# Subtractions that make the low halves of weights, and of sums of weights: from GpSimd to VectorE

## The chip, the cores and the metric

One NeuronCore of a Trainium2 chip runs the whole program. The time is that of one execution on the device in microseconds, and the kernel before was run three times: 880.67, 881.78 and 882.65 us, median 881.78.

## The reference

Three parts follow each other over 2304 tokens.

```python
phi = lambda x: exp(h - max(h)) / sqrt(m)        # h = x @ omega.T - |x|^2 / 2
num, den = phi(q) @ (phi(k).T @ v), phi(q) @ sum(phi(k))
x = num / (den + 1e-6)                           # attention, 4 x 8 heads, 576 x 64, 128 features
g = softplus(x @ w_in)                           # 512 -> 2048
y = g @ w_out                                    # 2048 -> 512
out = ((y @ w1) * (y @ w2)) @ w3 @ w_out2        # 512 -> 1024 -> 1024 -> 512
```

q and k are scaled by 64^(-1/4) first. All inputs and outputs are float32, and the products are wanted at that accuracy.

## The kernel before, in words

**Numbers in two halves.** Each operand of a large product is held as a high half (a cast to `float32r`) and a low half (the operand minus its high half), and a product is three matmuls: high by high, high by low, low by high (`mm3`, line 89; all matmuls carry line 87). The high half is a cast on ScalarE (`hi_` line 176, `hi_t` line 189, `dhi` line 581), the low half a subtraction: on GpSimd for the weights (`lo_` line 181), for the sums of weights (`lo_t` line 193) and for the attention's operands (`split`, line 263); on VectorE for the activations of the narrowing products (`dlo`, line 582), the activations of the widening ones (line 433) and the folded weight (line 794).

**Jobs.** A `Job` brings one block of weights in. It loads it as 64-bit words (line 120, issued from ScalarE's queue) and rebuilds the values from two 32-bit words: a `relu` on ScalarE (line 127), then four steps on VectorE (lines 130, 136, 143, 150), all in a tile `f` of the pool `T_`, which has four slots. The blocks of `w_in` (8 jobs) and of `w1` and `w2` (8 jobs, 1024 columns each) also get four sums of their quarters in a second tile `t` of that pool (lines 157, 160, 163), because the widening products go by a scheme with seven block products instead of eight. Such a job then makes `thi`, `tlo` (1024 columns), `hi`, and two pieces of `lo` (256 and 512 columns). The other jobs make `hi` and one `lo`: `w_out` (ten blocks of 768 columns and one of 512), `wo` (eight of 512, the last into the tile `spare`, line 715) and `w3` (eight of 1024). The halves lie in slots that come free when the matmuls of an earlier block are done.

**Stages.** Attention runs until about 155 us, and two jobs of `w_in` are done within it. The first widening product (`Up1`, from about 155 to 345 us) takes 24 quads, one for each block of `w_in` and third of the tokens; a quad has seven products of six matmuls, whose sums VectorE makes from PSUM (`add`, line 475: `u2`, `u3`, `c22`, `c21`, `c12`), which frees the banks, and ScalarE's softplus follows (line 507). The first narrowing product (`down`, lines 565 to 612, until about 575 us) multiplies 16 slices of `g` by `w_out` for five chunks of tokens; within it the jobs of `wo`, `w3` and six of `w1`/`w2` run (four of these only up to their values, which are spilled to memory and reloaded later), and `w3` is multiplied by `wo` (`fold`, line 719). The second widening product (`Up2`, until about 780 us) multiplies the two results by each other on VectorE (line 530: `c<-c,c` with both inputs in SBUF, `c<-ps,c` with one in PSUM), and the second narrowing product ends the kernel.

**What sets the order.** Job steps stand in a list `queue`; `step(rate)` (line 234) emits some of them after each product or slice, so that they are spread over the matmuls. A step that needs free slots waits for a count (`take`, line 105). In the list the step `lo_t` follows `hi_t`, then come `hi_` and `lo_`, and only then the next block's `relu` (lines 195 to 213). A scheduler of the framework then puts the instructions of each engine into one fixed order when the program is built, from program order and a plan of times; sums, softplus, `dhi`, `dlo` and results are marked urgent (`tc.high_priority(URGENT)`) and go ahead of what was emitted up to 300 places earlier if they are ready in that plan. On the chip every engine takes its instructions in that order, each after a wait for what it reads and for the slot that it writes.

Of the kernel before, what the change touches and what calls it, by code (L numbers as in the profile page):

```python
# [19 lines left out]
F32 = mybir.dt.float32  # L20
# [4 lines left out]
ALU = mybir.AluOpType  # L25
# [37 lines left out]
def body(ctx: ExitStack, tc: tile.TileContext, q, k, k_rest, v, v_rest, om_t, w_in, w_out, w12, w3, wo, out):  # L63
    nc = tc.nc
# [47 lines left out]
    class Job:  # L112
# [65 lines left out]
        def lo_(self):  # L178
            self.lo = self.place("lo")
            for a, b in ((0, 256), (512, 1024)) if self.sums else ((0, self.n),):  # L180
                nc.gpsimd.tensor_tensor(  # L181
                    out=self.lo[:, a:b], in0=self.f[:, a:b], in1=self.hi[:, a:b].bitcast(F32), op=ALU.subtract
                )
            self.done = True
# [5 lines left out]

        def lo_t(self):
            self.tlo = self.place("tlo")
            nc.gpsimd.tensor_tensor(out=self.tlo, in0=self.t, in1=self.thi.bitcast(F32), op=ALU.subtract)  # L193

        def splits(self):
            if self.sums:
# [686 lines left out]
```

## Time and profile before

| | us |
|---|---|
| median of three runs | 881.78 |
| lowest and highest | 880.67, 882.65 |
| the profiled execution | 882.83 |
| its span, first to last instruction | 881.0 |
| TensorE (PE) busy | 850.9 |
| VectorE (DVE) busy | 597.6 |
| ScalarE (ACT) busy | 381.8 |
| GpSimd (POOL) busy | 177.9 |

An engine's busy time is the time in which it runs instructions; those that only wait, branch or issue a DMA are not in it. A duration includes time in which a started instruction is held up. Idle time is put down to what ended it. The granted clock is a share of TensorE's full speed. Times in the views count from the start of the span.

### The profile page before, as it was taken

What the parts mean: (1) busy time and instruction counts of PE and PEld (TensorE: products, weight loads), DVE (VectorE), ACT (ScalarE), POOL (GpSimd) and SP (SyncE); (2) the same over time, 40 slices, a digit from 0 to 9 for tenths busy, and PEclk for the clock granted to TensorE, in tenths of its full rate; (3) what the DMA queues carried; (4) which work ended last, traced back from release to release, by engine and by line L of the source; (5) the groups of instructions that cost most, each with busy time, mean ns of one, the idle gap of its engine ahead of it and who ended that gap; (6) DMA issues with size and microseconds to landing.
All of it is one profiled execution on the core that took longest, in us unless ns stands there. A gap on an engine that the chain in (4) does not pass through costs nothing.

```text
span 881.0 us, 14617 instructions
## 1 busy us (share of the span) xinstructions
PE 850.9 (97%) x5496; PEld 763.9 (87%) x5496; DVE 597.6 (68%) x932; ACT 381.8 (43%) x796; POOL 177.9 (20%) x110
## 2 busy tenths in 40 slices
PE   8999989999899999999989999999999999999998
PEld 7888878989899988788768888899999999988887
DVE  5678788888775587887986686169986655563322
ACT  6678978563443455444433332164321111132221
POOL 3524420022222243222311211100042222000000
PEclk9999999999999999999989999999999999999999
DMA  8623534565443457766676664064322211364432
GB/s 298 240 84 97 156 99 133 186 215 181 156 149 133 150 195 266 239 190 237 203 275 235 238 219 161 31 204 137 126 102 78 78 54 55 128 201 144 143 120 96
DMA packets 72535, 141.68 MB, mean 161 GB/s; under 512 B 7056, under 2 KB 39952, under 8 KB 69392
## 3 DMA queue, kind: packets, MB, share of 16 engines
q1 hardware_dynamic: 65984, 102.99, 35.0%
q10 hardware_dynamic: 6480, 37.75, 12.5%
q8 instruction: 43, 0.70, 0.3%
q14 instruction: 28, 0.23, 0.1%
HBM read 94.05 MB, written 46.66 MB: 160 GB/s over the span
## 4 chain that ended last, share of the span: by engine, by line
PE 53%; DVE 4%; DMA 2%; issue 1%; ACT 1%; POOL 0%; ACTq 0%; DVEq 0%; POOLq 0%
PE ps L87 53%; DMA raw<-in_w 1%; DVE f L150 1%; DMA dn<-gd 1%; DVE f L143 1%; DVE dlo L582 0%; DVE f L130 0%; DMA raw<-in_wo 0%; DVE f L136 0%; ACT dhi L581 0%; DVE c L475 0%; DVE u L475 0%; ACT hi L176 0%; POOL tlo L193 0%; ACT f L127 0%
## 5 line engine op out<-in xcount | busy, mean ns | idle before, releaser
L181 POOL TENSOR_TENSOR lo<-f,hi 128x512 fp32r<-128x512 f32 (+3 forms) x58 | 93.2, 1621 | 195.1 <-ACT hi L176 162.5
L582 DVE TENSOR_TENSOR dlo<-dn,dhi 128x512 fp32r<-128x512 f32 (+1 forms) x120 | 89.0, 752 | 62.6 <-ACT dhi L581 44.1
L87 PE MATMUL ps<-dlo,hi 128*128 128x512 f32 (+1 forms) x320 | 120.8, 378 | 4.8 <-DVE dlo L582 4.8
L87 PE MATMUL ps<-dhi,hi 128*128 128x512 f32 (+1 forms) x320 | 119.1, 375 | 1.2 <-DVE c L475 0.7
L87 PE MATMUL ps<-dhi,lo 128*128 128x512 f32 (+1 forms) x320 | 120.2, 376 | 0.0
L193 POOL TENSOR_TENSOR tlo<-t,thi 128x1024 fp32r<-128x1024 f32 x16 | 39.7, 2478 | 301.6 <-ACT thi L189 195.5
L581 ACT CAST dhi<-dn 128x512 fp32r<-128x512 f32 (+1 forms) x120 | 67.3, 577 | 65.5 <-DVE dlo L582 30.7
L87 PEld LDWEIGHTS ps<-dlo,hi 128*128 128x128 f32 x320 | 60.8, 190 | 17.7 <-DVE dlo L582 6.2
L130 DVE SCALAR_TENSOR_TENSOR f<-raw,f 128x1024 f32<-128x1024 f32 (+2 forms) x43 | 51.0, 1188 | 33.2 <-ACT f L127 33.0
L87 PEld LDWEIGHTS ps<-dhi,hi 128*128 128x128 f32 x320 | 60.5, 189 | 14.6 <-DVE c L475 1.8
L475 DVE TENSOR_TENSOR c<-ps,u 128x384 f32<-128x384 f32 x144 | 71.6, 550 | 0.9
L87 PEld LDWEIGHTS ps<-dhi,lo 128*128 128x128 f32 x320 | 60.9, 190 | 11.7
L482 ACT COPY p<-ps 128x384 f32<-128x384 f32 x48 | 22.9, 477 | 103.8 <-PE ps L87 99.1
L475 DVE TENSOR_TENSOR u<-ps,p 128x384 f32<-128x384 f32 x48 | 26.6, 555 | 60.8 <-PE ps L87 60.8
L127 ACT ACTIVATE f<-raw 128x1024 f32<-128x1024 f32 (+2 forms) x43 | 42.5, 993 | 49.7 <-DMA raw<-in_w 25.4
L176 ACT CAST hi<-f 128x1024 fp32r<-128x1024 f32 (+2 forms) x42 | 38.5, 922 | 57.6 <-PE ps L87 30.8
L507 ACT ACTIVATE c<-c 128x384 f32<-128x384 f32 x72 | 35.2, 524 | 63.3 <-DVE c L475 59.0
L309 DVE TENSOR_REDUCE nmax<-ps 128x4 f32<-128x512 f32 x72 | 48.2, 683 | 19.4 <-PE ps L87 10.0
L87 PE MATMUL ps<-dlo,w34h 128*128 128x512 f32 (+1 forms) x160 | 59.6, 373 | 0.0
L87 PE MATMUL ps<-dhi,w34l 128*128 128x512 f32 (+1 forms) x160 | 59.6, 373 | 0.0
L87 PE MATMUL ps<-dhi,w34h 128*128 128x512 f32 (+1 forms) x160 | 59.1, 373 | 0.0
L150 DVE SCALAR_TENSOR_TENSOR f<-raw,f 128x1024 int32<-128x1024 int32 (+2 forms) x43 | 53.1, 1236 | 0.6
(147 smaller groups left out, 2163.5 us busy)
## 6 DMA issues: line engine op xcount, KB each, us to landing
gd<-c SPq DMA_DIRECT2D x96, 192.0 KB, 2.4
dn<-gd SPq DMA_DIRECT2D x64, 256.0 KB, 3.6
raw<-in_w ACTq DMA_DIRECT2D x16, 1024.0 KB, 6.0
pd<-c SPq DMA_DIRECT2D x48, 192.0 KB, 1.9
dn<-pd SPq DMA_DIRECT2D x32, 256.0 KB, 3.2
raw<-in_w_out ACTq DMA_DIRECT2D x10, 768.0 KB, 4.1
raw<-in_w_in ACTq DMA_DIRECT2D x6, 1024.0 KB, 5.0
rawq<-in_q SPq DMA_DIRECT2D x18, 256.0 KB, 3.8
```

The costliest lines, as they stand in the source:

```text
L87: nc.tensor.matmul(out=o, lhsT=a, rhs=b, start=start, stop=stop, **kw)
L127: nc.scalar.activation(out=self.f, in_=self.words(1, F32), func=AF.Relu, scale=-1.0)
L130: nc.vector.scalar_tensor_tensor(out=self.f, in0=self.words(1, F32), scalar=SMALLEST, in1=self.f, op0=ALU.max, op1=ALU.max)
L150: nc.vector.scalar_tensor_tensor(out=fi, in0=self.words(0, I32), scalar=29, in1=fi, op0=ALU.logical_shift_right, op1=ALU.bitwise_or,)
L176: nc.scalar.copy(out=self.hi, in_=self.f)
L181: nc.gpsimd.tensor_tensor(out=self.lo[:, a:b], in0=self.f[:, a:b], in1=self.hi[:, a:b].bitcast(F32), op=ALU.subtract)
L193: nc.gpsimd.tensor_tensor(out=self.tlo, in0=self.t, in1=self.thi.bitcast(F32), op=ALU.subtract)
L309: nc.vector.tensor_reduce(out=nmax, in_=pj, axis=AX.X, op=ALU.max, negate=True)
L475: nc.vector.tensor_tensor(out=z, in0=bank, in1=y, op=ALU.add)
L507: nc.scalar.activation(out=dst, in_=src, func=AF.Softplus)
L581: nc.scalar.copy(out=hi, in_=got[m])
L582: nc.vector.tensor_tensor(out=lo, in0=got.pop(m), in1=hi.bitcast(F32), op=ALU.subtract)
```

## The change

The subtractions `lo_` and `lo_t` of `Job` are issued on VectorE. Their operands, shapes, tiles and place in the list of steps are the same. The subtraction in `split`, line 263, stays on GpSimd.

```diff
--- before.py
+++ after.py
@@ -178,7 +178,7 @@
         def lo_(self):
             self.lo = self.place("lo")
             for a, b in ((0, 256), (512, 1024)) if self.sums else ((0, self.n),):
-                nc.gpsimd.tensor_tensor(
+                nc.vector.tensor_tensor(
                     out=self.lo[:, a:b], in0=self.f[:, a:b], in1=self.hi[:, a:b].bitcast(F32), op=ALU.subtract
                 )
             self.done = True
@@ -190,7 +190,7 @@
 
         def lo_t(self):
             self.tlo = self.place("tlo")
-            nc.gpsimd.tensor_tensor(out=self.tlo, in0=self.t, in1=self.thi.bitcast(F32), op=ALU.subtract)
+            nc.vector.tensor_tensor(out=self.tlo, in0=self.t, in1=self.thi.bitcast(F32), op=ALU.subtract)
 
         def splits(self):
             if self.sums:
```

## Rows read from the trace of the kernel before

**Rows 1.** The page: busy time, share and instructions of each engine over the span.

```profile
PE 850.9 (97%) x5496; PEld 763.9 (87%) x5496; DVE 597.6 (68%) x932; ACT 381.8 (43%) x796; POOL 177.9 (20%) x110
```

**Rows 2.** Busy time by stretch; then granted clock, DMA share and GB/s.

```profile
66.00:110.00 44.00, 43.32 (x586) 37.96 (x584) 35.12 (x91) 39.31 (x113) 20.48 (x15) 1.00 0.42 126
308.00:352.00 44.00, 41.19 (x219) 37.52 (x218) 36.23 (x52) 24.18 (x45) 16.30 (x8) 1.00 0.68 227
638.00:660.00 22.00, 21.22 (x122) 20.89 (x121) 19.60 (x33) 5.21 (x7) 10.18 (x6) 1.00 0.29 102
231.60:234.90 3.30, 3.30 (x12) 3.30 (x11) 2.45 (x5) 1.23 (x2) 0.00 (x0) 0.50 0.96 308
445.00:449.90 4.90, 4.90 (x12) 3.84 (x13) 3.29 (x4) 3.01 (x5) 2.37 (x1) 0.50 0.93 335
```

**Rows 3.** Timeline of TensorE: start, duration, instruction; in brackets idle time and what ended it.

```profile
230.08 0.45 PE L87 MATMUL ps<-xs1h,thi 128*128 128x384 f32 x1 [2.30 <-DVE c L475]
...
263.07 0.44 PE L87 MATMUL ps<-xs1h,thi 128*128 128x384 f32 x1 [1.55 <-DVE c L475]
...
287.13 0.44 PE L87 MATMUL ps<-xs1h,thi 128*128 128x384 f32 x1 [1.95 <-DVE c L475]
...
444.95 0.79 PE L87 MATMUL ps<-dlo,hi 128*128 128x512 f32 x1 [4.30 <-DVE dlo L582]
...
641.39 0.45 PE L87 MATMUL ps<-xs2h,tlo 128*128 128x384 f32 x1 [0.78 <-POOL tlo L193]
```

**Rows 4.** GpSimd by line and shape: count, busy us, mean ns; idle time before.

```profile
L193 POOL TENSOR_TENSOR tlo<-t,thi 128x1024 fp32r<-128x1024 f32 x16 | 39.7, 2478 | 301.6 <-ACT thi L189 195.5 <-PE ps L87 106.2
L181 POOL TENSOR_TENSOR lo<-f,hi 128x512 fp32r<-128x512 f32 x24 | 36.3, 1511 | 29.7 <-ACT hi L176 29.7
...
L181 POOL TENSOR_TENSOR lo<-f,hi 128x768 fp32r<-128x768 f32 x10 | 20.5, 2064 | 40.0 <-ACT hi L176 26.3 <-PE ps L87 13.6
L181 POOL TENSOR_TENSOR lo<-f,hi 128x1024 fp32r<-128x1024 f32 x8 | 20.4, 2553 | 90.3 <-ACT hi L176 71.3 <-PE ps L87 13.4 <-issue 5.5
L181 POOL TENSOR_TENSOR lo<-f,hi 128x256 fp32r<-128x256 f32 x16 | 16.7, 1045 | 35.1 <-ACT hi L176 35.1
```

**Rows 5.** VectorE by line and shape, forms that show an unhindered duration.

```profile
L143 DVE SCALAR_TENSOR_TENSOR f<-raw,f 128x1024 int32<-128x1024 int32 x24 | 29.4, 1225 | 0.4
...
L160 DVE TENSOR_TENSOR t<-f,t 128x256 f32<-128x256 f32 x16 | 6.7, 420 | 0.2
...
L433 DVE TENSOR_TENSOR xa22l<-xq,xa22h 128x768 fp32r<-128x768 f32 x6 | 5.7, 950 | 0.0
...
L794 DVE TENSOR_TENSOR w34l<-w,w34h 128x512 fp32r<-128x512 f32 x8 | 5.4, 687 | 5.1 <-ACT w34h L791 5.1
```

**Rows 6.** The same view of VectorE, three long forms and one to compare.

```profile
L582 DVE TENSOR_TENSOR dlo<-dn,dhi 128x512 fp32r<-128x512 f32 x96 | 79.4, 834 | 52.8 <-ACT dhi L581 39.1 <-PE ps L87 10.2 <-DMA wd<-w 3.0
...
L130 DVE SCALAR_TENSOR_TENSOR f<-raw,f 128x1024 f32<-128x1024 f32 x24 | 33.8, 1408 | 16.6 <-ACT f L127 16.5
...
L530 DVE TENSOR_TENSOR c<-c,c 128x384 f32<-128x384 f32 x24 | 21.8, 906 | 0.0
...
L530 DVE TENSOR_TENSOR c<-ps,c 128x384 f32<-128x384 f32 x24 | 13.2, 551 | 0.0
```

**Rows 7.** Timeline of VectorE and GpSimd at two places: start, duration, instruction.

```profile
224.58 3.43 POOL L193 TENSOR_TENSOR tlo<-t,thi 128x1024 fp32r<-128x1024 f32 x1 [11.62 <-ACT thi L189]
...
226.13 2.96 DVE L150 SCALAR_TENSOR_TENSOR f<-raw,f 128x1024 int32<-128x1024 int32 x1
...
438.05 2.99 DVE L130 SCALAR_TENSOR_TENSOR f<-raw,f 128x1024 f32<-128x1024 f32 x1
```

**Rows 8.** Timeline of ScalarE in the first widening product.

```profile
283.32 0.90 ACT L127 ACTIVATE f<-raw 128x768 f32<-128x768 f32 x1 [3.07 <-POOL lo L181]
```

**Rows 9.** VectorE by line and shape in the stretch 308 to 352 us.

```profile
L130 DVE SCALAR_TENSOR_TENSOR f<-raw,f 128x768 f32<-128x768 f32 x6 | 7.2, 1215 | 4.6 <-ACT f L127 4.5
L150 DVE SCALAR_TENSOR_TENSOR f<-raw,f 128x768 int32<-128x768 int32 x5 | 7.0, 1401 | 0.1
```

## The prediction

> **What bounds the kernel now.** I read the page's busy times first: TensorE is busy 850.9 of 881.0 us, VectorE 597.6, GpSimd 177.9 [rows 1]. So the time is TensorE's work plus 30.1 us in which it stands still; only that, and stretches in which its clock is low, can be won, while VectorE has 283 us to spare on the whole. Then I read stretches [rows 2] and the places where TensorE waits [rows 3]. Of the 30.1 us, 12.8 sit in the first widening product (2.30, 1.55, 1.95 us, and a second of the 1.95 kind one job, 24 us, later: four stalls, all ended by a sum on line 475 that frees a PSUM bank), at the end of the first narrowing product (4.30 us, ended by a low half on line 582) and at the start of the second widening one (0.78 us, ended by GpSimd's own `tlo`) [rows 3]. The other 17 are the two ends of the kernel, the attention stage and the first operands, and I leave them as they are. After two of them the granted clock is 0.50, the lower of its two levels (1.2 instead of 2.4 GHz), in at least 3.3 and 4.9 us of work [rows 2]; before each fall TensorE had stood still for over 2 us.
>
> **What is moved.** 16 sums of weights (1024 columns), and of line 181: 16 of 256, 24 of 512, 10 of 768 and 8 of 1024 columns [rows 4], with one more of 512 into the `spare` tile: 75 instructions. No DMA moves, no queue is changed but these two. GpSimd loses 39.7 + 36.3 + 20.5 + 20.4 + 16.7 = 133.6 us and keeps only the splits of line 263. On VectorE a subtraction of two SBUF tensors takes 0.687 us for 512 columns, 0.950 for 768 and 0.420 for 256; for 1024 there is no subtraction, and the nearest is line 143, two SBUF inputs as well, 1.225 [rows 5]. Added to VectorE: 24 x 1.225 + 25 x 0.687 + 10 x 0.950 + 16 x 0.420 = 29.4 + 17.2 + 9.5 + 6.7 = 62.8 us.
>
> **What VectorE gets back.** Some of its instructions are longer than others of their shape. `dlo` at 512 columns averages 834 ns where the same operation on line 794, in a stretch without GpSimd, takes 687: 96 x 0.147 = 14.1 us. `c<-c,c` averages 906 where `c<-ps,c`, with one input in PSUM, takes 551: 24 x 0.355 = 8.5. Line 130 at 1024 columns averages 1408 against 1225: 4.4 [rows 5, 6]. In the stretch 308 to 352 the 768-column forms of lines 130 and 150 average 1215 and 1401 against 950: 6 x 0.265 + 5 x 0.451 = 3.8 [rows 9]. The single rows say when: line 150 at 226.13 takes 2.96 us while GpSimd's `tlo`, begun at 224.58, runs to 228.01; line 130 at 438.05 takes 2.99 [rows 7]. VectorE is held while GpSimd reads SBUF. Together 30.8 us at least come back, so VectorE's busy time grows by at most 32 us, to about 629: by itself that reaches nothing on the path.
>
> **What it does to TensorE's stalls, one by one.**
> - At 227.8 to 230.1: line 150 stands directly ahead of the sums that free the bank. Alone it takes 1.22, so they come 1.74 us earlier. A stall of 0.6 should leave the clock up: half of the 3.3 us at 0.50 comes back as well, 1.65 [rows 2, 3, 7]. Gain 3.4; bounds 0 (a moved `tlo` of 1.22 takes the freed place) and 4.0 (2.30 and the clock).
> - At 261.5 and twice as at 285.2: here the chain runs over tile slots. ScalarE's `relu` for the next job waits for the slot that GpSimd's low half still reads (3.07 us at 283.32 [rows 8]), line 130 on VectorE waits for `relu`, and the sums that TensorE needs are queued behind line 130. A `tlo` is 2.48 - 1.23 = 1.25 shorter on VectorE, the two `lo` 1.05 + 1.51 - 0.42 - 0.69 = 1.45 [rows 4, 5]. I take 1.2 of the 1.55, and both 1.95 whole, as 1.25 + 1.45 is more: 5.1. Bounds 0 and 5.45.
> - At 440.7: the VectorE order is line 130 (2.99), 136, 143, 150 and then the `dlo` that TensorE waits for. The hold of 1.77 goes, a `lo` of 1.22 comes in: 0.5 gained. Bounds: -1.2 (no hold goes, the `lo` comes), and 4.30 + 4.9 x 0.5 = 6.7 if the stall and its low clock go altogether [rows 2, 3, 7].
> - At 640.6: `tlo` itself is what TensorE waits for. It is shorter, but must now find a place between VectorE's urgent sums; I take 0, bounds +0.8 (the stall goes) and -1.1 (three sums and two products of 0.55 us, overlapping to 2.4 us, go ahead of it, less the 1.25).
>
> **What it costs.** In the attention stage two jobs are split, 2 x (1.225 + 0.420 + 0.687) = 4.7 us more on VectorE, where it is 80% busy and TensorE almost full (35.1 and 43.3 of 44 us [rows 2]). Cover is thin; I take 2.0, bounds 0 and 4.7. Every moved instruction follows a cast on ScalarE, and now all of VectorE's queue stands behind it if the cast is late. GpSimd could wait there at no cost. The nearest rows for that: 0.0 behind the operand cast (line 433) and 5.1 us over 8 (0.64 each) on line 794 [rows 5]; for 59 casts that is 0 to 38 us of VectorE idling, out of 283, and I cost it at 0 where TensorE has work in hand, since the urgent sums are ordered ahead. If that cover goes, the next late thing is a sum on line 475 again.
>
> Sum: -3.4 - 5.1 - 0.5 + 0 + 2.0 = -7.0 us. The profiled execution took 882.83 (span 881.0 and 1.8 around it), 1.05 above the median 881.78. So 881.8 - 7.0 = **874.8 us**.
>
> **Rivals.** *VectorE becomes the bound in the stages where it is full* (slower). 308 to 352 holds eight 768-column halves: 36.2 + 7.6 = 43.8 of 44 us if the held time did not come back, 40.0 with the 3.8 of [rows 2, 9]; 638 to 660 two jobs: 19.6 + 4.7 = 24.3 of 22. The mechanism: in each job of the first widening product the `tlo`, behind its cast, stands ahead of the sums that free the banks, in the very place that the hold leaves. Then the four stalls stay and each of the six jobs there adds 1.22: +7.3, with the 2.0 of the attention stage +9.3, so 891; it decides from the point where the wait of the `xs1h` matmuls for line 475 is above 2.3 us per job. For it: the stalls are there now, with VectorE not full. Against it: the hold cannot be foreseen by an order fixed at build time, while a planned instruction can. The Trainium skill has a rule on this side (Perfetto Trace Analysis, Optimizing Scalar/DVE Operations): "if DVE is saturated, offloading some work to Scalar (or even GPSIMD) may make sense", though it adds that between those two it might not help because they share a read port; by the first half the time would come out as in this rival, by the second as in my sum, and the lengthened rows speak for the second.
>
> *The late stall goes too* (faster). The 1024-column jobs ahead of 438 lose holds like the 1.77 there, the `dlo` comes in time and the clock stays up: another 6.7 - 0.5 = 6.2 off, 868.6. For it: 4.30 us of stall behind one held instruction. Against it: four job instructions stay queued ahead of that `dlo`, and a fifth joins them.
>
> *Nothing to measure.* Only the hold at 226 counts (-3.4), attention and the start at 640 take 2.0 and 1.1 back: 881.5. The slot chain would then be followed by the next wait, `relu` for its load.
>
> **Chances.** My forecast 0.46, the late stall gone too 0.19, nothing 0.13, VectorE the bound 0.22. About 0.2% (1.8 us) is what a measurement of this kernel can tell from no change. So faster 0.65, same 0.13, slower 0.22. The likeliest case alone spans 871 to 879, from the bounds of attention (0 to 4.7) and of 440 and 640. The range goes down to 866, past the 868.6 by the bounds of the first two stalls, and up to 887, which takes in half of the slower rival.
>
> **What would show it.** Right: GpSimd down to about 43 us; VectorE 615 to 630; `dlo` at 512 columns near 690 ns and `c<-c,c` near 550; no stall over 1 us in 200 to 310, no 0.50 clock near 231; line 127 no longer waiting for a low half. Wrong: stalls ended by line 475 as long as before, with a moved subtraction ahead of the sum; long idling of VectorE ahead of `lo` or `tlo` for a cast; or new stalls with a low clock in 308 to 352 or 638 to 660.

## The result, and the profile after

The changed kernel took 868.15 us (median of six runs, 865.56 to 873.72), the kernel before 881.43 us in its six runs beside it: a ratio of 0.985, with an interval of [0.9829, 0.9871], so 13.2 us less. A second set of runs on another chip gave 868.18 against 883.39, 0.9817 [0.9791, 0.9843], 16.1 us less. The ratios are taken over all runs of both kernels and differ a little from those of the medians. From here on a difference in us is a ratio's distance from 1 times 882, so 0.001 is 0.9 us.

The profiled execution took 865.56 us, with a span of 863.7; it is the shortest of the six, so the two traces lie 17.3 us apart and not 13.2. Its busy times, on the page:

```profile
PE 845.2 (98%) x5496; PEld 760.6 (88%) x5496; DVE 605.7 (70%) x1007; ACT 381.8 (44%) x796; POOL 43.5 (5%) x35
```

Against [rows 1], GpSimd lost 134.4 us and VectorE gained 8.1, for 75 instructions. TensorE's idle time fell from 30.1 to 863.7 - 845.2 = 18.5 us, by 11.6 of those 17.3 us; its work at the low clock, where half the time is lost, went from 8.5 us (near 231 and after 443) to 6.8.

VectorE by line and shape (count, busy us, mean ns, idle before), to set against [rows 5, 6]:

```profile
L582 DVE TENSOR_TENSOR dlo<-dn,dhi 128x512 fp32r<-128x512 f32 x96 | 65.4, 689 | 50.3 <-ACT dhi L581 28.2 <-PE ps L87 13.9 <-issue 5.9
L130 DVE SCALAR_TENSOR_TENSOR f<-raw,f 128x1024 f32<-128x1024 f32 x24 | 30.1, 1255 | 22.6 <-ACT f L127 22.6
...
L193 DVE TENSOR_TENSOR tlo<-t,thi 128x1024 fp32r<-128x1024 f32 x16 | 19.6, 1228 | 9.4 <-ACT thi L189 9.4
L181 DVE TENSOR_TENSOR lo<-f,hi 128x512 fp32r<-128x512 f32 x24 | 16.5, 686 | 1.3 <-ACT hi L176 1.3
L136 DVE TENSOR_SCALAR f<-f 128x1024 int32<-128x1024 int32 x24 | 16.4, 686 | 0.2
...
L530 DVE TENSOR_TENSOR c<-c,c 128x384 f32<-128x384 f32 x24 | 13.2, 549 | 0.0
L181 DVE TENSOR_TENSOR lo<-f,hi 128x1024 fp32r<-128x1024 f32 x8 | 9.8, 1222 | 0.8 <-ACT hi L176 0.8
...
L181 DVE TENSOR_TENSOR lo<-f,hi 128x768 fp32r<-128x768 f32 x10 | 9.5, 950 | 2.1 <-ACT hi L176 2.1
...
L181 DVE TENSOR_TENSOR lo<-f,hi 128x256 fp32r<-128x256 f32 x16 | 7.5, 467 | 2.8 <-ACT hi L176 2.8
```

The moved work is 19.6 + 16.5 + 9.8 + 9.5 + 7.5 = 62.9 us, and 0.7 for `spare`. What pays for it stands in the other rows: `dlo` 689 ns instead of 834, `c<-c,c` 549 instead of 906, line 130 1255 instead of 1408.

TensorE by stretch (busy PE, PEld, DVE, ACT, POOL, granted clock, DMA share, GB/s). The work that the kernel before has at 440 to 462 and at 638 to 660 runs at about 432 to 448 and 623 to 645 here, so the last two stretches are set earlier than in [rows 2]:

```profile
66.00:110.00 44.00, 41.94 (x522) 36.10 (x523) 35.10 (x89) 34.23 (x96) 11.36 (x9) 0.96 0.35 107
198.00:308.00 110.00, 110.00 (x637) 110.00 (x636) 89.54 (x144) 52.38 (x99) 0.00 (x0) 1.00 0.54 183
308.00:352.00 44.00, 39.81 (x191) 34.25 (x190) 39.10 (x57) 23.54 (x40) 0.00 (x0) 0.96 0.68 232
426.00:448.00 22.00, 22.00 (x96) 17.73 (x95) 16.09 (x20) 9.05 (x14) 0.00 (x0) 1.00 0.88 290
622.70:644.70 22.00, 22.00 (x129) 22.00 (x128) 20.89 (x39) 5.44 (x7) 0.00 (x0) 1.00 0.30 102
```

Every stall of [rows 3] is gone. In 198 to 308, where the kernel before has PE busy for 104.20 of 110 us, it never stops, and there is no low clock near 231 or where the stall of 440 was. But two stretches of the first half are worse than they were, and in both the clock is now at 0.96. The timeline of TensorE shows the stalls that are new:

```profile
88.39 1.10 PE L368 MATMUL ps<-ident,qp 128*128 128x128 f32 x4 [1.26 <-ACT qp L314]
...
341.92 0.50 PE L87 MATMUL ps<-dlo,hi 128*128 128x512 f32 x1 [2.22 <-DVE dlo L582]
```

After each of them the clock was 0.50 for 3.4 us (from 90.5 and from 343.1). The second trace of this kernel (e12_after) has both stalls again, 1.26 and 2.21 us, but no low clock behind the first. The stall at 339.7 is a price of the change, as the timelines of ScalarE and VectorE ahead of it show:

```profile
337.84 1.14 ACT L581 CAST dhi<-dn 128x512 fp32r<-128x512 f32 x2
...
338.45 0.95 DVE L181 TENSOR_TENSOR lo<-f,hi 128x768 fp32r<-128x768 f32 x1
339.32 0.95 DVE L143 SCALAR_TENSOR_TENSOR f<-raw,f 128x768 int32<-128x768 int32 x1
340.30 0.96 DVE L150 SCALAR_TENSOR_TENSOR f<-raw,f 128x768 int32<-128x768 int32 x1
341.18 1.29 DVE L582 TENSOR_TENSOR dlo<-dn,dhi 128x512 fp32r<-128x512 f32 x2
```

`dhi` was ready at 338.98, but `dlo` began at 341.18. A moved `lo` and two steps of the next job stood ahead of it on VectorE, none of them lengthened.

### The profile page after: what moved, and what is told of

The parts are those of the page before. It is cut to its first block, busy times and chain, and to the rows that moved or that the text cites. A ratio compares the mean times of both kernels' runs of the same rounds, so it can differ in the third digit from the quotient of the medians.

```text
span 863.7 us, 14514 instructions
## 1 busy us (share of the span) xinstructions
PE 845.2 (98%) x5496; PEld 760.6 (88%) x5496; DVE 605.7 (70%) x1007; ACT 381.8 (44%) x796; POOL 43.5 (5%) x35
## 4 chain that ended last, share of the span: by engine, by line
PE 81%; DVE 4%; DMA 3%; issue 1%; ACT 1%; SPq 0%; DVEq 0%; ACTq 0%
PE ps L87 80%; DMA xq<-xd 2%; PE ps L368 1%; PE ps L398 1%; DMA raw<-in_w_in 1%; DVE s L423 1%; DVE c L475 0%; DMA dn<-gd 0%; DMA gd<-c 0%; DVE f L143 0%; DVE u L475 0%; DVE nmax L309 0%; DVE xt L389 0%; DVE lo L181 0%; DVE dlo L582 0%
## 5 line engine op out<-in xcount | busy, mean ns | idle before, releaser
L582 DVE TENSOR_TENSOR dlo<-dn,dhi 128x512 fp32r<-128x512 f32 (+1 forms) x120 | 74.8, 636 | 60.2 <-ACT dhi L581 33.5
L482 ACT COPY p<-ps 128x384 f32<-128x384 f32 x48 | 22.8, 475 | 99.5 <-PE ps L87 78.0
L130 DVE SCALAR_TENSOR_TENSOR f<-raw,f 128x1024 f32<-128x1024 f32 (+2 forms) x43 | 45.7, 1066 | 27.0 <-ACT f L127 26.9
L309 DVE TENSOR_REDUCE nmax<-ps 128x4 f32<-128x512 f32 x72 | 48.1, 682 | 18.5 <-PE ps L87 11.9
L181 DVE TENSOR_TENSOR lo<-f,hi 128x512 fp32r<-128x512 f32 (+3 forms) x58 | 42.0, 745 | 6.9 <-ACT hi L176 6.9
L143 DVE SCALAR_TENSOR_TENSOR f<-raw,f 128x1024 int32<-128x1024 int32 (+2 forms) x43 | 45.3, 1056 | 0.6
L150 DVE SCALAR_TENSOR_TENSOR f<-raw,f 128x1024 int32<-128x1024 int32 (+2 forms) x43 | 44.9, 1046 | 0.4
```

The costliest lines, as they stand in the source:

```text
L130: nc.vector.scalar_tensor_tensor(out=self.f, in0=self.words(1, F32), scalar=SMALLEST, in1=self.f, op0=ALU.max, op1=ALU.max)
L143: nc.vector.scalar_tensor_tensor(out=fi, in0=self.words(1, I32), scalar=-0x40000000, in1=fi, op0=ALU.bitwise_and, op1=ALU.bitwise_or,)
L150: nc.vector.scalar_tensor_tensor(out=fi, in0=self.words(0, I32), scalar=29, in1=fi, op0=ALU.logical_shift_right, op1=ALU.bitwise_or,)
L181: nc.vector.tensor_tensor(out=self.lo[:, a:b], in0=self.f[:, a:b], in1=self.hi[:, a:b].bitcast(F32), op=ALU.subtract)
L309: nc.vector.tensor_reduce(out=nmax, in_=pj, axis=AX.X, op=ALU.max, negate=True)
L582: nc.vector.tensor_tensor(out=lo, in0=got.pop(m), in1=hi.bitcast(F32), op=ALU.subtract)
```

## The experiments

All of them were run in five rounds beside the kernel before. The theory was that GpSimd holds VectorE up while it reads SBUF, and that this delay, not the duration of GpSimd's own work, is what TensorE's stalls were made of. The main rival was the chain of slots: a low half on GpSimd keeps `f` or `t` longer, so that `relu` and all that follows it start late.

### Reading or only writing: e3_again and e8_hold

Both are the changed kernel with GpSimd work put behind each moved subtraction: in the one GpSimd reads SBUF (it takes the low half from itself, which leaves zeros), in the other it only writes, and keeps the slot that much longer.

```diff
 # e3_again, behind each lo (and the same with tlo)
+nc.gpsimd.tensor_tensor(out=self.lo[:, a:b], in0=self.lo[:, a:b].bitcast(F32),
+                        in1=self.lo[:, a:b].bitcast(F32), op=ALU.subtract)
 # e8_hold, behind each lo (and the same with t)
+nc.gpsimd.memset(self.f[:, a:b], 0.0)
```

> The changed kernel, with one GpSimd subtraction of the old shape added behind each moved one: it takes the finished low half from itself in place, so the low halves of the weights are zero here and those terms are left out of the output. It reads SBUF as the old GpSimd work did, but not the tiles f and t, so ScalarE's relu does not wait for it. Theory 'hold' (VectorE is held while GpSimd reads SBUF, and that delayed the sums and dlo): dlo and the bit steps again reach 2.5 to 3.0 us, VectorE's busy time rises by 30 to 45 us, and at least 5 of the 13 us are lost: 873 to 882. Rival 'slots' (what cost time was the slow release of the four slots of f and t): relu still doesn't wait, 866 to 871 whatever VectorE's durations do.

> The changed kernel, with a GpSimd memset over f and over t behind each moved subtraction. It only writes, and keeps each slot of f and t some 1 us longer, about as long as the old GpSimd subtraction did. The output is the full one. Theory 'hold': two-input VectorE instructions keep their unhindered durations (dlo near 690 ns) and the time stays at 866 to 870. Rival 'slots': relu waits for GpSimd again, stalls of 1 to 2 us of TensorE between 200 and 310 us return, 873 to 878.

With the reads: 881.04 us, 0.9973 [0.9952, 0.9994], so nearly all that the change had won was gone. Its page, and two rows of VectorE by line and shape:

```profile
PE 849.1 (97%) x5496; PEld 761.2 (87%) x5496; DVE 654.7 (75%) x1007; ACT 381.9 (44%) x796; POOL 161.1 (18%) x110
```

```profile
L582 DVE TENSOR_TENSOR dlo<-dn,dhi 128x512 fp32r<-128x512 f32 x96 | 68.8, 726 | 40.4 <-ACT dhi L581 26.8 <-PE ps L87 8.7 <-issue 4.7
L130 DVE SCALAR_TENSOR_TENSOR f<-raw,f 128x1024 f32<-128x1024 f32 x24 | 32.9, 1370 | 17.0 <-ACT f L127 17.0
```

GpSimd was busy 117.6 us more than in the changed kernel, and VectorE, with the same 1007 instructions, 49.0 us more (30 to 45 had been expected). Timelines of GpSimd, VectorE and TensorE at the longest new stall:

```profile
348.33 2.11 POOL L183 TENSOR_TENSOR lo<-lo 128x768 fp32r<-128x768 f32 x1 [5.62 <-DVE lo L181]
...
349.15 2.10 DVE L150 SCALAR_TENSOR_TENSOR f<-raw,f 128x768 int32<-128x768 int32 x1
...
351.91 0.80 PE L87 MATMUL ps<-dlo,hi 128*128 128x512 f32 x1 [3.35 <-DVE dlo L582]
```

Line 150 took 2.10 us here, under GpSimd's read, against 0.96 at 340.30 in the changed kernel, and it stood ahead of the `dlo` that TensorE wanted. Three things have to be said against this run, though. Some 55 of VectorE's 1007 places in the order differ from the changed kernel. At 198.25 TensorE waits 0.95 us for GpSimd's second `tlo` itself. And most of the time was lost at other places than those where the change had won it (TensorE by stretch):

```profile
198.00:308.00 110.00, 108.31 (x610) 107.10 (x609) 96.47 (x140) 51.28 (x95) 27.92 (x18) 1.00 0.48 165
308.00:352.00 44.00, 35.94 (x188) 31.75 (x186) 41.72 (x55) 21.53 (x39) 13.29 (x8) 1.00 0.67 226
```

None of the four stalls near 230 to 310 came back, nor that of 440; 308 to 352, where PE is busy 39.81 us in the changed kernel and 41.19 in the kernel before, lost more than any other stretch. So the run shows that GpSimd's reads lengthen VectorE's instructions and that this can cost as much as the change had won. It does not show what the stalls of the kernel before were made of.

With the writes alone: 867.77 us, 0.9823 [0.979, 0.9857], the time of the changed kernel. VectorE was busy 606.9 us, with 16 places in its order changed. Two rows by line and shape:

```profile
L582 DVE TENSOR_TENSOR dlo<-dn,dhi 128x512 fp32r<-128x512 f32 x96 | 65.2, 688 | 46.9 <-ACT dhi L581 27.0 <-PE ps L87 11.5 <-issue 5.5
...
L193 POOL MEMSET t<- 128x1024 f32 x16 | 15.3, 956 | 325.2 <-DVE tlo L193 325.2
```

So 48.2 us of GpSimd work that only writes lengthened the instructions with two SBUF inputs by next to nothing; line 136, which has a single tensor input, gained some 1.0 us in all (703 instead of 686 ns at 1024 columns). A slot kept about 1 us longer cost nothing in the changed kernel, but from 198 to 310 us no `relu` waited for it either, so the run does not tell what the longer keeping cost in the kernel before. The Trainium skill (SBUF — State Buffer, Who interferes with whom) has the same division: a VectorE instruction with two SBUF inputs contends with a GpSimd instruction that reads SBUF, and not with one that only writes it. These two runs agree with it: `dlo` 726 and 688 ns.

### A shorter read in the same order: e4_nochain and e10_chain

Both are the kernel before, with GpSimd taking the high half twice instead of the value and the high half (so the low halves are zero). In e4_nochain `f` and `t` come free with the casts; e10_chain adds a one-column `memset` of them behind each, which ties them to GpSimd again.

```diff
-out=self.lo[:, a:b], in0=self.f[:, a:b], in1=self.hi[:, a:b].bitcast(F32), op=ALU.subtract
+out=self.lo[:, a:b], in0=self.hi[:, a:b].bitcast(F32), in1=self.hi[:, a:b].bitcast(F32), op=ALU.subtract
 # e10_chain only
+nc.gpsimd.memset(self.f[:, a:a + 1], 0.0)
```

> The kernel before, with GpSimd's subtraction reading the high half twice in place of f (or t) and the high half: same engine, shape and reads of SBUF, but f and t are free as soon as the cast on ScalarE is done. The low halves of the weights are zero and those terms are left out. Theory 'hold' alone: VectorE's long durations stay, the stall at 440 us with its low clock stays, at most 1 to 3 us are won: 878 to 881. Rival 'slots': the three stalls that my working put down to slots (5.1 us) go, 872 to 877. If both are at work, something between, 875 to 879.

> The kernel e4_nochain (GpSimd subtracts the high half from itself) with one more GpSimd instruction behind each subtraction: a memset of one column of f or t, so that the slots of f and t are again free only when GpSimd is done. VectorE's instructions stand in the very order of the kernel before. The low halves of the weights are zero here. Theory 'slots' (on GpSimd the late release of the slots is what costs, through relu and what is queued behind it on VectorE): the 13 us that e4_nochain won are lost again, 879 to 884, relu waits 2 to 3 us for GpSimd and the four stalls near 230 to 310 us are back. Rival 'lighter reads' (e4_nochain was faster because GpSimd reads one tensor and not two, 2.0 against 2.5 us, and so holds VectorE less): 867 to 872.

e4_nochain took 869.06 us, 0.9838 [0.9804, 0.9872], faster than all its forecasts. It did more than cut the chain: GpSimd is faster when both operands are the same tensor, as the row of the second run shows too, 1983 ns for `tlo` against 2478 [rows 4]:

```profile
L193 POOL TENSOR_TENSOR tlo<-thi 128x1024 fp32r<-128x1024 f32 x16 | 31.7, 1983 | 303.6 <-ACT thi L189 175.2 <-PE ps L87 128.4
```

e10_chain took 873.03 us, 0.9904 [0.9875, 0.9933], between its two forecasts. It is the cleaner one, as every VectorE instruction stands in the order of the kernel before. The low halves of the jobs took GpSimd 110.5 us instead of 134.9 (the 133.6 of the prediction and 1.3 for `spare`), VectorE was busy 581.0 instead of 597.6, and the six stalls of the kernel before are all there and all shorter (timeline of TensorE):

```profile
227.49 0.44 PE L87 MATMUL ps<-xs1h,thi 128*128 128x384 f32 x1 [1.55 <-DVE c L475]
...
257.84 0.44 PE L87 MATMUL ps<-xs1h,thi 128*128 128x384 f32 x1 [0.96 <-DVE c L475]
...
281.06 0.45 PE L87 MATMUL ps<-xs1h,thi 128*128 128x384 f32 x1 [1.11 <-DVE c L475]
...
304.28 0.44 PE L87 MATMUL ps<-xs1h,thi 128*128 128x384 f32 x1 [1.10 <-DVE c L475]
...
435.69 0.50 PE L87 MATMUL ps<-dlo,hi 128*128 128x512 f32 x1 [2.36 <-DVE dlo L582]
...
630.62 0.44 PE L87 MATMUL ps<-xs2h,tlo 128*128 128x384 f32 x1 [0.40 <-POOL t L193]
```

Against 2.30, 1.55, 1.95, 4.30 and 0.78 [rows 3], and 1.92 for the fourth,

```profile
311.16 0.44 PE L87 MATMUL ps<-xs1h,thi 128*128 128x384 f32 x1 [1.92 <-DVE c L475]
```

that is 5.3 us of the 8.5 that the run gained; the low clock near 231 went as well, and that after 440 lasted 3.4 us instead of 6.8. So the length of GpSimd's reads sets the stalls, in an order that is the same: by the holds, by the slots that a shorter read frees sooner, or by both. Between the two runs lie 5.8 us, for slots that come free early, for the one-column writes, and for the some 150 of 932 places by which e4_nochain's order differs. In the kernel before the chain of slots therefore very likely counts too; how holds and slots share the 20.6 us of the last group was not separated further.

### Place by place: e5_win, e6_down, e9_w12

Each moves one group of the 75 instructions alone and leaves the rest on GpSimd: the 24 of `w_in`; the 27 of `w_out`, `wo` and `w3`; the 24 of `w1` and `w2`.

```diff
-nc.gpsimd.tensor_tensor(
+(nc.vector if self in win else nc.gpsimd).tensor_tensor(        # e5_win
+(nc.vector if not self.sums else nc.gpsimd).tensor_tensor(      # e6_down
+(nc.vector if self in w12_j else nc.gpsimd).tensor_tensor(      # e9_w12
```

> The kernel before with the moved subtractions on VectorE for the eight blocks of w_in alone (8 tlo, 16 lo). If the gain lies where I placed it, this is the first widening product's part: 7.7 us of stalls less what remains, and 1.7 of low clock, less up to 2 in attention: 873 to 876, with TensorE full from 198 to 308 us. If the gain needs GpSimd to be empty everywhere, 878 to 882.

> The kernel before with the moved subtractions on VectorE for w_out, wo and w3 alone (27 lo). It should take the stall of 4.3 us at 440 and its low clock (2.4 us) away and leave the four stalls of 227 to 310 us: 875 to 878. If the stall at 440 is one of order and not of GpSimd, 879 to 882.

> The kernel before with the moved subtractions on VectorE for the eight blocks of w1 and w2 alone (8 tlo, 16 lo). Only the 0.78 us at 640 hang on these: 880 to 882.5, which a measurement can hardly tell from no change. If VectorE, 89% busy from 638 to 660 us, cannot take them, 883 to 886.

| kernel | us | ratio | less |
|---|---|---|---|
| e5_win | 875.46 | 0.9912 [0.9884, 0.994] | 7.8 |
| e6_down | 876.06 | 0.9931 [0.9905, 0.9956] | 6.1 |
| e9_w12 | 880.89 | 0.9977 [0.9956, 0.9999] | 2.0 |

The parts add up to 15.9 us, between the 13.2 and the 16.1 of the whole, and each takes away the stalls of its own stretch. In e5_win the four stalls between 227 and 311 us are gone and TensorE is full from 198 to 308; one of 1.35 us has come at the end of the first widening product, and the one of 440 is there (timeline of TensorE):

```profile
323.89 0.45 PE L87 MATMUL ps<-xs1h,thi 128*128 128x384 f32 x1 [1.35 <-DVE c L475]
...
436.99 0.50 PE L87 MATMUL ps<-dlo,hi 128*128 128x512 f32 x1 [3.79 <-DVE dlo L582]
```

In e6_down it is the other way round; the first and the last of its four stalls:

```profile
229.88 0.44 PE L87 MATMUL ps<-xs1h,thi 128*128 128x384 f32 x1 [3.04 <-DVE c L475]
...
311.14 0.44 PE L87 MATMUL ps<-xs1h,thi 128*128 128x384 f32 x1 [1.91 <-DVE c L475]
```

In e9_w12 the stall of 440 measures 4.41 us; that of 640 is gone.

### What the work costs on VectorE: e11_none, e12_after, e13_att, e14_mix, e7_split

e11_none is the kernel before with a `memset` in place of each subtraction: GpSimd reads nothing there, VectorE has none of the work, slots are free with the casts, and a low half does not wait for its cast. e13_att and e14_mix put groups of the changed kernel back on GpSimd, e7_split moves line 263 to VectorE as well, e12_after is the changed kernel again.

```diff
 # e11_none, against the kernel before
-nc.gpsimd.tensor_tensor(out=self.lo[:, a:b], in0=self.f[:, a:b], in1=self.hi[:, a:b].bitcast(F32), ...)
+nc.gpsimd.memset(self.lo[:, a:b].bitcast(F32), 0.0)
 # against the changed kernel
-nc.vector.tensor_tensor(
+(nc.gpsimd if self in win[:2] else nc.vector).tensor_tensor(                      # e13_att
+(nc.gpsimd if self in win[:2] or self.n == 768 else nc.vector).tensor_tensor(     # e14_mix
 # e7_split, in split, line 263
-nc.gpsimd.tensor_tensor(out=lo, in0=f, in1=hi.bitcast(F32), op=ALU.subtract)
+nc.vector.tensor_tensor(out=lo, in0=f, in1=hi.bitcast(F32), op=ALU.subtract)
```

> The kernel before, with a memset by GpSimd into the low half in place of each moved subtraction: the low halves of all weights and of their sums are zero, GpSimd writes and reads nothing there, the tiles f and t come free with the casts, and VectorE has none of the moved work. Theory (GpSimd's reading is the whole cost, VectorE has room for the 62.8 us): 864 to 868, that is 0 to 4 us under the changed kernel; VectorE busy 535 to 550, that is 605.7 less 62.8 and little else, and dlo at 512 columns near 690 ns. Rival (the moved work costs on the path as well, and the change wins 13 us only net of that): 856 to 863.

> The changed kernel again, unaltered, on the same chip as the other two: 866 to 870 in every theory; the other two are compared with this one.

> The changed kernel, with the low halves of the first two jobs of w_in, those that are split within the attention stage, on GpSimd as before. The prediction's term for the attention stage (+2.0): 866.2, that is 2 us under the changed kernel. Rival (that stage has cover enough for 4.7 us of VectorE's work): 867 to 870, no difference.

> The changed kernel, with two groups of low halves back on GpSimd: the first two jobs of w_in (split within the attention stage) and the ten 768-column blocks of w_out (split around the change from the first widening to the first narrowing product, where a moved subtraction stands ahead of a dlo that TensorE waits for, 2.22 us at 339.70 in the changed kernel). Theory A (that stall is the price of the moved work there and GpSimd's holds in this stretch cost less): the stall goes with its low clock, 3 to 4 us, and 1 to 2 us in the attention stage: 862 to 865, a ratio to the kernel before of 0.976 to 0.980. Theory B (the holds of the 768-column forms, 3.8 us in rows 9, take the place of the moved work): a stall of the same size at another place near 340, 866 to 869, 0.981 to 0.985. Theory C (the stall at 440 comes back, as its jobs go by the same queue): 870 to 874, 0.986 to 0.990.

> The changed kernel with the attention's split subtraction (line 263) on VectorE too, so that GpSimd computes nothing there. VectorE gets 18 x 0.687 + 6 x 1.225 + 4 x 0.42 + 0.42, about 22 us, in the first 155 us, and loses what those 29 GpSimd instructions still hold it for (6 to 8 us). Theory 'hold': where VectorE is fullest (66 to 154 us, some 84%) this about evens out: 864 to 871. Rival 'VectorE is the bound in attention': its added 15 us show on TensorE there, 872 to 880.

| kernel | us | ratio | less |
|---|---|---|---|
| e11_none | 863.09 | 0.9767 [0.9742, 0.9793] | 20.6 |
| e12_after | 868.18 | 0.9817 [0.9791, 0.9843] | 16.1 |
| e13_att | 866.18 | 0.9801 [0.9784, 0.9818] | 17.6 |
| e14_mix | 865.67 | 0.9801 [0.9775, 0.9827] | 17.6 |
| e7_split | 868.44 | 0.9841 [0.9805, 0.9876] | 14.0 |

The first three ran on the same chip. So GpSimd's subtractions, by holds, slots and their own lateness together, cost the kernel before 20.6 us (18.3 to 22.8), and doing them on VectorE costs some 4.4 us back (by the two ratios; their intervals just touch, so this is likely and not certain). The forecast of e11_none by the theory was 864 to 868, its rival's 856 to 863: it came out at the border, and both say something true. VectorE's busy time in it was 554.1 us, where 535 to 550 had been expected. That is 43.5 us under the kernel before, about what GpSimd's reading added there, and 51.6 under the changed kernel, what the moved work fills; the difference is the 8.1 us by which VectorE's busy time grew.

```profile
PE 843.8 (98%) x5496; PEld 760.7 (88%) x5496; DVE 554.1 (64%) x932; ACT 382.2 (44%) x796; POOL 90.1 (10%) x110
```

The place of the 4.4 us can be seen. The narrowing product from its first `dhi,hi` to its last takes 331.3 to 580.5, 249.2 us, in e11_none, and 253.7 us in the changed kernel (330.4 to 584.1; 253.7 in e12_after as well), which has the 2.22 us at 339.7 and half of 3.4 us of low clock behind it. In the kernel before it takes 341.7 to 598.5, so the 575 us given further up for its end were too early.

e13_att, without the moved work in the attention stage, is 1.4 us under e12_after, but the intervals overlap: by the times, the forecast of 2 us is neither shown nor excluded. In the traces the first widening product begins at 150.4 us in e13_att and at 150.7 and 149.0 in the two of the changed kernel, so no cost ahead of it can be seen. e14_mix was to take the stall at 339.7 away as well. That stall went, and two others came, which stand in e5_win too, where `w_out` is also on GpSimd (timelines of GpSimd, VectorE and TensorE; the profiled execution was the longest of the five):

```profile
325.31 0.44 PE L87 MATMUL ps<-xs1h,thi 128*128 128x384 f32 x1 [1.34 <-DVE c L475]
...
336.19 1.85 POOL L181 TENSOR_TENSOR lo<-f,hi 128x768 fp32r<-128x768 f32 x1 [9.68 <-ACT hi L176]
...
336.69 1.76 DVE L136 TENSOR_SCALAR f<-f 128x768 int32<-128x768 int32 x1
...
340.96 0.65 PE L87 MATMUL ps<-dhi,hi 128*128 128x512 f32 x1 [2.23 <-DVE c L475]
```

That is its theory B: there a hold (line 136 takes 1.76 us beside GpSimd's `lo`, and 0.55 on average in the changed kernel) takes the place of the moved work, 2.23 for 2.22 us of stall. The time lies on the border of A and B and cannot be told from that of e13_att or of the changed kernel; no version here that makes the low halves is measurably better than the change itself.

e7_split left GpSimd 0.7 us of work and brought nothing over the changed kernel. The first widening product began at 144.7 us instead of 150.7, but its operands weren't there (timeline of TensorE):

```profile
170.49 0.44 PE L87 MATMUL ps<-xs2h,thi 128*128 128x384 f32 x1 [2.47 <-ACT xs2h L430]
172.24 0.69 PE L87 MATMUL ps<-xs2l,thi 128*128 128x384 f32 x1 [1.30 <-DVE xs2l L433]
...
175.50 0.69 PE L87 MATMUL ps<-xs3h,thi 128*128 128x384 f32 x1 [1.30 <-ACT xs3h L430]
```

With 10.2 us of low clock behind these stalls (half of it lost), all of the 6 us was given back: the narrowing product began at 331.4 us, in the changed kernel at 330.4.

## Why the prediction was right, and where it was not

The direction and the mechanism held, and the size was too small: 7.0 us forecast, 13.2 and 16.1 measured. The time, 868.15, is that of the rival "the late stall goes too" (868.6), below the 871 to 879 that the likeliest case spanned. That it lies so near 868.6 is partly luck: two of that rival's terms came out better, the first widening product (10.7 us won in the traces, 8.5 forecast) and the attention stage (no cost to be seen, 2.0 forecast), and they make up for the 3.9 us lost at 340, for which its sum had no term.

- **What is moved.** 62.8 us were forecast and 63.6 measured, GpSimd at 43.5 us. The nearest rows for each shape were good to 0.3%, but for the 256-column piece, 467 ns instead of 420: two of the 16 lie in the attention stage, beside GpSimd's splits, and take 798 there.
- **What comes back.** "30.8 us at least" was a floor far too low, as about 43.5 came back: VectorE's busy time grew by 8.1 us, not up to 32, and 605.7 lies under the 615 to 630 named. The three terms by name were right (`dlo` 14.0 for 14.1, `c<-c,c` 8.6 for 8.5, line 130 3.7 for 4.4). Missing were the other forms that were too long, lines 136, 143, 150, 423 and 262, and VectorE's short instructions overlap their neighbours, so that 63.6 us of them fill 51.6. Line 136 at 1024 columns, 686 ns here, has a single tensor input and still took 831 in e3_again.
- **The first widening product.** 3.4 + 5.1 = 8.5 us forecast, 7.8 [5.3, 10.2] in e5_win alone; all four stalls gone and no low clock near 231. From its first matmul (`xs2h,thi`) to the first `dhi,hi` the product takes 179.7 us instead of 190.4 in the traces, 10.7 less. `relu` waits for no low half any more: the view of line 127 in 198 to 310 us has nothing under "sat idle".

```profile
L127 ACT ACTIVATE f<-raw x10: 907/923/1146, 207.3 to 309.4; 128x768 f32<-128x768 f32 x6, 128x1024 f32<-128x1024 f32 x4
...
its engine sat idle before it (us, times) until:
who waited for it (us, times):
  ACT c L507: 4.5, 1
  DVE f L130: 3.8, 3
```

- **The stall at 440: the step that failed.** The prediction took one hold of 1.77 us off and put one `lo` of 1.22 in, a gain of 0.5. e6_down, which moves the jobs of that stretch alone, gained 6.1 us [3.9, 8.4], near the upper bound of 6.7 (the stall and its low clock altogether). The step looked at the one held instruction that was visible in the last 3 us, and not at the jobs ahead of it, which were late by their own holds; that they were is what the rival "the late stall goes too" said. The kernel before shows one of them on VectorE:

```profile
428.47 2.54 DVE L582 TENSOR_TENSOR dlo<-dn,dhi 128x512 fp32r<-128x512 f32 x1 [1.03 <-ACT dhi L581]
```

From it to the `dlo` that TensorE waited for VectorE had no pause, so this hold (2.54 less 0.69) and that of line 130 add up to 3.6 of the 4.30 us. e10_chain supports it: in the same order, with GpSimd's reads a fifth shorter, this stall alone shrank by 1.94 us.
- **The start at 640.** 0 was forecast, within -0.8 and +1.1; the stall of 0.78 went, and e9_w12 gained 2.0 [0.1, 3.9]. The place between the urgent sums that `tlo` might not find was there: over the same work (622.7 to 644.7 us) VectorE was busy 20.89 us of 22, and not 24.3. That more than the 0.78 was won there is not shown.
- **The attention stage.** +2.0 was forecast. The change brought a new stall of 1.26 us there. It stands in all five traces that have the low halves of those two jobs on VectorE and the splits of line 263 on GpSimd, and in no other; a low clock follows it in three of them. Other stalls went: the first widening product began at 150.7 us, and at 149.0 in e12_after, instead of 151.2. e13_att leaves 1.4 us with overlapping intervals. A cost can't be shown.
- **VectorE's queue behind the casts.** 0 to 38 us of idling were allowed, and 9.4 + 1.3 + 0.8 + 2.1 + 2.8 = 16.4 stand in the rows of the moved forms; TensorE was busy through all of it.
- **The slower rival.** Its mechanism is real at one place: 308 to 352, which it had named as the full stretch (40.0 of 44 us forecast; 39.10 now, and 39.33 from 297 to 341, where most of the same work runs), with a moved `lo` ahead of a `dlo`. It cost 3.9 us, not 9.3. In the first widening product, where it was to decide, it did not: TensorE stopped nowhere in 110 us. Of the two halves of the rule in the Trainium skill (Perfetto Trace Analysis, Optimizing Scalar/DVE Operations) that the prediction quoted, the second held here: offloading to GpSimd helped less (some 4.4 us) than it hindered (20.6). VectorE, 68% busy, was not saturated, so the first half was not put to the test.

## What to carry to other kernels

Price an engine's work by what it does to its neighbour as well as by its own time: here 133.6 us of GpSimd subtractions, which TensorE itself waited for only once (0.78 us), cost 20.6 us, in the main through the lengthened instructions of VectorE and the slots that they kept, and the same work on a VectorE that was already 68% busy cost some 4.4. To see it in a profile, look for one form of instruction with two mean durations, and collect every form that has them, not only the largest. And where a stall stands behind one lengthened instruction, count the holds of the whole queue ahead of it: the last one is only the part that can be seen.

## What was not expected of the hardware

- GpSimd's work that only writes SBUF (`memset`, 48.2 us more of it in e8_hold) lengthened VectorE's busy time by 1.2 us (`dlo` 688 ns), while 117.6 us of reading in e3_again lengthened VectorE's busy time by 49.0 us.
- GpSimd subtracts a tensor from itself faster than from another: 1983 against 2478 ns on average for 1024 columns (e10_chain and [rows 4]), and 1893 against 2357 for the shortest of each.
- TensorE's clock fell to 0.50 after a stall of 1.26 us (at 90.5 in the changed kernel), though the stalls of 1.55, 1.95 and 1.92 us in the first widening product before (two of them in [rows 3]) had no such fall behind them: the clock there is 1.00 from 262 to 325. The same stall of 1.26 us had a fall behind it in two other runs (e5_win, e8_hold) and none in e12_after and e3_again, and one of 3.03 us in e9_w12 (at 230.1) had none. The prediction had read off two falls that each followed a stall of over 2 us; by these rows the length of the stall before it does not settle whether the clock falls.
